# A three-stage attention and feed-forward kernel: one transpose for the leftover keys of two query parts, quarter tiles in the fifth value step, and another order of all operations

## The chip, the cores and the metric

The kernel runs on one core of a Trainium2 chip. TensorE (PE in the rows; its weight loads are PEld) multiplies matrices, VectorE (DVE), ScalarE (ACT) and GpSimd (POOL) work elementwise, and SyncE (SP) issues most transfers. The metric is the device time of one execution in microseconds (us), the median of several runs.

## The reference, cut to what matters

```python
scores = scale * np.matmul(q, k.transpose(0, 1, 3, 2))      # 4 batches, 8 heads, 576 queries and keys, head size 64
thresh = np.max(scores, axis=-1, keepdims=True) - tau
scores = np.where(scores >= thresh, scores, -1000000000.0)
attn = np.exp(scores - np.max(scores, axis=-1, keepdims=True))
attn = attn / (np.sum(attn, axis=-1, keepdims=True) + 1e-09)
x = np.matmul(attn, v)                    # laid out as 2304 tokens x 512
h = x @ moe_w_in;   x = (h * np.clip(h + 3, 0, 6) / 6) @ moe_w_out                 # 512 -> 2048 -> 512
h = x @ moe2_w_in;  out = (h * (1 / (1 + np.exp(-1.702 * h)))) @ moe2_w_out        # 512 -> 2048 -> 512
```

## The kernel before

The kernel writes its work down as some five thousand operations, each with an engine, a planned cost, its buffers and a function that issues its instructions (`add`, `move`, class `Plan`). Many operations have an alternative engine (`alt`). `Plan.settle` runs a list scheduler over them: `order` keeps, for each engine, a heap sorted by a key, and starts whatever comes first and is ready by the planned costs and the latencies `LAT`. The emitted program is the operations in the order of their planned starts. Each engine then executes its own list strictly in that order, and semaphores keep the dependencies. The costs are the writer's formulas: a one-input GpSimd operation on n columns is put at `pool1(n)`, 124 + 1.042 n nanoseconds. In the kernel before, two long lists of seeds (`KICKS`, `SHAKES`) disturb the key and swap engines until the final order comes out.

Attention works in units of two heads, four units to a batch. Batch 0 (`half`) is worked differently from batches 1 to 3 (`full`), which the change touches: 12 units in all. The 576 queries of a head are two parts, p = 0 with 256 queries and p = 1 with 320 (`CH`). One tile of scores is 128 queries by 576 keys. A unit has nine: two tiles for each head in each part, and a ninth (number 4, `tiles[4]` is None) with the last 64 queries of both heads. `score2` multiplies a tile on TensorE (L685); `soft` finds its maximum (DVE L733), the threshold (L734 or ACT L735), the exponentials (ACT L736), and masks and sums (DVE L737). `norm` multiplies the whole 576-column tile by the reciprocal sum (L750 on GpSimd, L753 on VectorE).

The weighted sum over values needs the keys on the partitions, so that the tiles have to be turned. 576 keys are four blocks of 128 and a leftover of 64. In part 0 (`blocks`) VectorE turns 32 by 32 blocks of the first 512 keys (L802) and two rounds of transfers finish the turn; in part 1 (`turn`) TensorE transposes them, 128 by 128 at a time (L791). The leftover 64 keys of the four tiles of each part go through TensorE in both parts: four transposes with 64 output rows, and one copy out of PSUM (L794 on ScalarE, L795 on VectorE). The upper 64 rows of the target are zeroed once for all units (L1246, L1247). Then `av_` multiplies (L850): for each part five steps of 128 keys (the fifth half zeros), and in each step one multiplication for each of the two heads. A head has 64 value columns, so the two heads lie side by side in the array. The names: `e` and `er` are tiles of attention weights (er the ninth), `et` the turned weights, `kqv` a buffer of keys, queries or values, `pm` a PSUM bank, `xr` the result.

Between and after these units run the two feed-forward layers in split form (a high and a low part of each operand, three multiplications a product): L910, L935, L1025 and L1136. Their weights arrive as 64-bit numbers and are decoded by `decode`: ScalarE takes the magnitude (L528), then a maximum and a minimum are applied (L529 on VectorE, or its alternative L530 on GpSimd), VectorE shifts (L531) and adds the sign (L532), GpSimd adds the low word, and `split` makes the high and low parts (`inhring`, `inlring`, `outhring`, `outlring`). The staging tile is `wmstg`. L478 and L475 are helper lines that many elementwise operations share. Where the planner leaves TensorE idle, `fill` puts in dummy multiplications (L1303).

```python
        def pool1(n):
            return 124 + 1.042 * n
...
        add(DVE, 335, time, "W", lambda: nc.vector.tensor_scalar(out=t.t, in0=t.t, scalar1=2.0 ** -15, scalar2=MOST, op0=ALU.max, op1=ALU.min), [], [t], (),
            (POOL, pool1(DM), lambda: nc.gpsimd.tensor_scalar(out=t.t, in0=t.t, scalar1=2.0 ** -15, scalar2=MOST, op0=ALU.max, op1=ALU.min)))
```

Of the kernel before, what the change touches and what calls it, by code (L numbers as in the profile page):

```python
# [9 lines left out]
F32 = mybir.dt.float32  # L10
# [8 lines left out]
P = 128  # L19
# [12 lines left out]
PORT = {DVE: {"W", "XHB", "XLB", "XD", "XLC", "GT2", "GL", "qs", "N", "kl", "XL", "XH", "GH", "kh", "qh", "ql"}, POOL: {"kl", "qs", "ql", "vl", "W", "GD", "N", "RM", "EL", "XL", "XLC", "GL"}}  # L32

KICKS = (
    1066518432, 520434182, 607402147, 51636981, 155525685, 845670547, 33034277, 701254722, 228382444, 659205109,
)

SHAKES = (
# [67 lines left out]
class Plan:  # L106
# [145 lines left out]
    def latest(self):  # L252
# [27 lines left out]
        return out  # L280

    def settle(self):

        self.link()
        self.order([float(o.time) for o in self.ops])
        for _ in range(3):
            key = self.latest()
            length = self.order(key)
# [43 lines left out]
def kicked(key, length, seed, kinds, count, ref=None):  # L332
# [6 lines left out]
    for _ in range(4):  # L339
        draw()  # L340
# [1021 lines left out]
```

## Time and profile before

| | |
|---|---|
| median of 3 runs | 1057.41 us (1056.98 to 1058.03) |
| span of the profiled execution, first to last instruction | 1054.9 us |
| TensorE busy | 1040.5 us (99%) |
| VectorE, ScalarE, GpSimd busy | 754.5, 618.5, 493.0 us |

The profiled execution has no time of its own beside its span; the three runs lie 2.1 to 3.1 us above that span, which is what starting and ending an execution adds outside the first and the last instruction. An engine's busy time is the union of its instructions. A matmul of full 32-bit numbers shows as two instructions of TensorE, a transpose as one. An instruction's duration contains its pipeline, so that neighbours overlap: what one costs on the path is the distance from its start to that of the next.

### The profile page before, as it was taken

The numbers are of one execution on the slowest core, as the hardware profiler recorded it, in microseconds if no ns is written. First come the engines' busy times: TensorE is split into PE (matmuls) and PEld (weight loads), VectorE is DVE, ScalarE is ACT, GpSimd is POOL, SyncE is SP. The second block draws the span as 40 slices with busy tenths as digits, with TensorE's granted clock in tenths as the row PEclk, the third lists the DMA queues.
The fourth block names the chain that finished last, engine by engine and source line by source line (L and its number), as shares of the span: only waits on it lengthen the run. The fifth ranks groups of instructions, "written<-read, shape, count | busy, mean of one in ns | idle before, by whom it ended". The sixth has DMA issues, their size and how long they took to land.

```text
span 1054.9 us, 19387 instructions
## 1 busy us (share of the span) xinstructions
PE 1040.5 (99%) x7066; PEld 948.2 (90%) x7066; DVE 754.5 (72%) x1539; ACT 618.5 (59%) x1228; POOL 493.0 (47%) x556
## 2 busy tenths in 40 slices
PE   8999999999999999999999999999999999999998
PEld 6686888899889998999999999989988998989988
DVE  7999889867888883677786426997687587464544
ACT  5989676566656664666454215655765566345433
POOL 5687877666757662755564226432331232001000
PEclk9999999999999999999999999999999999999999
DMA  7334465645564535445644213446553342321302
GB/s 231 121 113 137 147 181 162 183 137 160 161 184 132 148 115 162 137 144 167 203 145 145 84 43 111 135 139 200 165 191 120 125 159 78 115 88 33 96 2 74
DMA packets 83647, 141.71 MB, mean 134 GB/s; under 512 B 8160, under 2 KB 47712, under 8 KB 82016
## 3 DMA queue, kind: packets, MB, share of 16 engines
q1 hardware_dynamic: 83408, 140.18, 44.1%
q8 instruction: 56, 0.92, 0.4%
q14 instruction: 39, 0.32, 0.1%
q10 hardware_dynamic: 144, 0.29, 0.1%
HBM read 97.32 MB, written 43.12 MB: 133 GB/s over the span
## 4 chain that ended last, share of the span: by engine, by line
PE 88%; DVE 4%; ACT 2%; DMA 2%; SPq 1%; POOL 1%; issue 1%; DVEq 0%; ACTq 0%; POOLq 0%
PE py L935 26%; PE pm L1136 17%; PE pm L910 10%; PE pm L935 9%; PE pm L1025 7%; PE ps L685 6%; PE pm L850 6%; PE pm L791 4%; PE ps L717 1%; PE pm L833 1%; DMA kqv<-in_vp_dram 1%; DVE wmstg L532 1%; ACT et L794 1%; SPq L644 0%; DVE nm L733 0%
## 5 line engine op out<-in xcount | busy, mean ns | idle before, releaser
L935 PE MATMUL py<-g,outhring 128*128 128x512 f32 (+3 forms) x1024 | 279.1, 357 | 1.7 <-DVE yc L478 1.6
L935 PEld LDWEIGHTS py<-g,outhring 128*128 128x128 f32 x1024 | 178.0, 188 | 17.9 <-DVE yc L478 2.1
L935 PE MATMUL py<-g,outlring 128*128 128x512 f32 (+3 forms) x512 | 182.5, 356 | 0.0
L1136 PE MATMUL pm<-outhring,inhring 128*128 128x256 f32 x512 | 144.4, 282 | 0.0
L1136 PE MATMUL pm<-outlring,inhring 128*128 128x256 f32 x512 | 144.1, 282 | 0.2 <-DVE outlring L478 0.2
L1136 PE MATMUL pm<-outhring,inlring 128*128 128x256 f32 x512 | 143.9, 281 | 0.0
L733 DVE TENSOR_REDUCE nm<-ps 128x1 f32<-128x576 f32 x144 | 106.9, 752 | 31.1 <-PE ps L685 27.2
L478 POOL TENSOR_TENSOR wmstg<-wmstg,wrstg 128x512 uint32<-128x512 uint32 x48 | 68.0, 1417 | 93.3 <-DVE wmstg L532 59.5
L736 ACT ACTIVATE e<-ps,nm 128x576 f32<-128x576 f32 x128 | 93.0, 739 | 31.4 <-DVE nm L733 27.4
L737 DVE SCALAR_TENSOR_TENSOR e<-ps,th,e 128x576 f32<-128x576 f32 x128 | 102.3, 811 | 12.4 <-ACT e L736 9.9
L478 POOL TENSOR_TENSOR g<-t,g 128x256 fp32r<-128x256 f32 (+2 forms) x83 | 78.5, 952 | 65.3 <-ACT g L475 49.9
L478 POOL TENSOR_TENSOR g<-tc,g 128x512 fp32r<-128x512 f32 x24 | 32.0, 1334 | 164.2 <-ACT g L475 139.4
L935 PE MATMUL pm<-g,outhring 128*128 128x256 f32 (+1 forms) x512 | 106.9, 300 | 0.1
L935 PEld LDWEIGHTS py<-g,outlring 128*128 128x128 f32 x512 | 96.2, 188 | 11.0
L1136 PEld LDWEIGHTS pm<-outlring,inhring 128*128 128x128 f32 x512 | 96.8, 189 | 4.3 <-DVE outlring L478 0.5
L1136 PEld LDWEIGHTS pm<-outhring,inhring 128*128 128x128 f32 x512 | 96.7, 189 | 4.0
L910 PE MATMUL pm<-xh,inhring 128*128 128x256 f32 (+1 forms) x320 | 97.5, 305 | 0.2
L1136 PEld LDWEIGHTS pm<-outhring,inlring 128*128 128x128 f32 x512 | 97.5, 190 | 0.0
L910 PE MATMUL pm<-xh,inlring 128*128 128x256 f32 (+1 forms) x320 | 94.4, 295 | 0.0
L910 PE MATMUL pm<-xl,inhring 128*128 128x256 f32 (+1 forms) x320 | 94.4, 295 | 0.0
L935 PEld LDWEIGHTS pm<-g,outhring 128*128 128x128 f32 x512 | 82.0, 189 | 1.4 <-issue 0.9
L685 PE MATMUL ps<-kqv 128*128 128x288 f32 x480 | 81.2, 300 | 0.0
(139 smaller groups left out, 2453.9 us busy)
## 6 DMA issues: line engine op xcount, KB each, us to landing
turned<-tr SPq DMA_DIRECT2D x12, 1024.0 KB, 4.2
et<-turned SPq DMA_DIRECT2D x48, 256.0 KB, 6.3
wrawstg<-in_w1i_dram SPq DMA_DIRECT2D x16, 512.0 KB, 3.9
wrawstg<-in_w1o_dram SPq DMA_DIRECT2D x16, 512.0 KB, 3.6
wrawstg<-in_w2i_dram SPq DMA_DIRECT2D x16, 512.0 KB, 4.0
wrawstg<-in_w2o_dram SPq DMA_DIRECT2D x16, 512.0 KB, 3.7
qk<-in_k_dram SPq DMA_DIRECT2D x24, 288.0 KB, 4.1
qk<-in_q_dram SPq DMA_DIRECT2D x24, 288.0 KB, 3.6
```

The lines of the kernel that those rows point to most:

```text
L478: return lambda: (nc.vector if eng == DVE else nc.gpsimd).tensor_tensor(out=o(), in0=a(), in1=b(), op=op)
L532: add(DVE, 602, time, "W", lambda: nc.vector.scalar_tensor_tensor(out=tu(), in0=high(), scalar=0xC0000000, in1=tu(), op0=ALU.bitwise_and, ...
L685: nc.tensor.matmul(ps.t[:, i, :SH], qss[hd].t[:, q0:q0 + P], w[hd].t[:, i * SH:(i + 1) * SH], start=a, stop=z)
L733: add(DVE, 672, K("R", s), "R", lambda: nc.vector.tensor_reduce(out=nm.t[:, c], in_=ps.t[:, :, :SH], op=ALU.max, axis=AX.XY, negate=True), ...
L736: add(ACT, 624, K("X", s), "X", lambda: nc.scalar.activation(out=ev(), in_=ps.t[:, :, :SH], func=ACTF.Exp, bias=nm.t[:, c]), [ps, (nm, s)] ...
L737: add(DVE, 736, K("M", s), "M", lambda: nc.vector.scalar_tensor_tensor(out=ev(), in0=ps.t[:, :, :SH], scalar=th.t[:, c], in1=ev(), op0=ALU ...
L791: nc.tensor.transpose(pt.t[:kn, o:o + P], e_of[s].t[:, keys(k)], id_b.t)
L850: nc.tensor.matmul(pv[p].t[64 * hd:64 * hd + 64, :CH[p][1]], v_(k, hd), x, start=k == 0, stop=k == 4)
L910: nc.tensor.matmul(ph.t[:, :n], a, v, start=(cc == 0 and i == 0), stop=(cc == KC - 1 and i == 2))
L935: nc.tensor.matmul(py.t[:, :n], a, v, start=(st and i == 0), stop=(sp and i == 2))
L1025: nc.tensor.matmul(ph.t[:, :n], a, v, start=(cc == 0 and q == 0), stop=(cc == KC - 1 and q == 2))
L1136: nc.tensor.matmul(o.t[:, :n], u.t[:, ws], v.t[:, xv], start=(st and kk == 0 and i == 0), stop=(sp and kk == 1 and i == 2), skip_group_che ...
```

## The change

It has three parts. The line numbers behind an arrow are those of the changed kernel.

First, the leftover keys. In the 12 units of batches 1 to 3, `norm` no longer multiplies the whole tile at once: it does the first 512 columns in place and writes the last 64 columns into a packed buffer `pk` (L750 -> L784), in which the leftovers of a tile of part 0 and of the corresponding tile of part 1 lie side by side as 128 columns. `packed` transposes `pk` with four full transposes, so that part 0's leftover keys come out on partitions 0 to 63 and part 1's on 64 to 127. The two groups of four 64-row transposes, one for each part, become one group of four, and two copies out of PSUM become one. The ninth tile's leftover is transposed with the 64 keys before it, so that it lands on partitions 64 to 127. The two memsets of zeros go.

Second, the fifth value step. `av_` does four steps for each part as before (L850 -> L927), then four multiplications at the end (L931), each with 64 keys and 64 value columns, that is a quarter of the array: part 0 on partitions 0 to 63, part 1 on 64 to 127, the two heads on the two halves of the columns. Each of the two parts still has its own PSUM bank.

Third, the order. The seeds are replaced by a list of operations whose engine is swapped (`SWAPS`) and a table of ranks (`RANKS`), by which the same list scheduler sorts. Every engine's whole list changes. The program has 48 matmuls less (6,631 before, 6,583 now). Among the swaps: the maximum and minimum of the decoded weights stands on GpSimd 22 times (3 before) and on VectorE 42 times (61 before), the multiplication of the first 512 columns on ScalarE for 38 of 96 tiles, the thresholds on ScalarE 56 times (26 before), and the low parts of g on GpSimd 60 times (83 before). The counts of transfers are the same. `TURNED` is empty, so that `both` is False and part 1 is turned by TensorE (`turned_by_pe`) in every unit, as before.

```diff
...
+RANKS = """
...
+SWAPS = (
+    18, 22, 28, 33, 58, 68, 108, 128, 148, 168, 192, 197, 254, 259, 269, 274, 316, 326, 331, 360, 371, 393, 410, 430, 453, 517, 528, 542, 615, 619, 629, 633, 659, 667, 669, 683, 692,
...
     def settle(self):
...
+        for n in SWAPS:
+            op = self.ops[n]
+            (op.eng, op.cost, op.fn), op.alt = op.alt, (op.eng, op.cost, op.fn)
...
-        self.link()
+        key = [float(o.time) for o in self.ops]
+        ranks = b85decode("".join(RANKS.split()))
+        if ranks:
+            key = [float(ranks[i] + 256 * ranks[i + 1]) for i in range(0, len(ranks), 2)]
         self.order(key)
+        for _ in range(0 if ranks else 3):
+            self.order(self.latest())
         return sorted(self.ops, key=lambda o: (self.start[o.n], o.n))
...
     def et_4():
-        return ets[1].t[:, 2048:2560].rearrange("p (h n) -> p h n", h=2)
+        return ets[1].t[:, 2048:2688].rearrange("p (h n) -> p h n", h=2)
...
+        pk = None if early else buf("pk", 2, "tr", [P, 4, 2, 64])
...
             recip(ss, ss[-1])
             for s in ss:
-                def mul(s=s, e=e_of[s]):
-                    nc.gpsimd.tensor_scalar(out=e.t, in0=e.t, scalar1=rc.t[:, s:s + 1], scalar2=1.0, op0=ALU.mult, op1=ALU.mult)
-
-                def alone(s=s, e=e_of[s]):
-                    nc.vector.tensor_scalar(out=e.t, in0=e.t, scalar1=rc.t[:, s:s + 1], scalar2=1.0, op0=ALU.mult, op1=ALU.mult)
-
-                add(POOL, 724, K("N", ss[-1]), "N", mul, [(rc, s)], [e_of[s]], (), (DVE, 69 + 0.521 * S, alone))
+                t, e = tiles[s], e_of[s]
+
+                def mul(eng, o, i, s=s):
+                    return lambda: (nc.vector if eng == DVE else nc.gpsimd).tensor_scalar(out=o(), in0=i(), scalar1=rc.t[:, s:s + 1], scalar2=1.0, op0=ALU.mult, op1=ALU.mult)
+
+                n = 512 if t else S
+
+                def main(e=e, n=n):
+                    return e.t[:, :n]
+
+                add(POOL, pool1(n), K("N", ss[-1]), "N", mul(POOL, main, main), [(rc, s)], [(e, 0)] if t else [e], (),
+                    (ACT, act(n), lambda main=main, s=s: nc.scalar.activation(out=main(), in_=main(), func=ACTF.Copy, scale=rc.t[:, s:s + 1])))
+                if t:
+                    def to(t=t):
+                        return pk.t[:, 2 * t[0] + t[1] % 2, t[1] // 2]
+
+                    def of(e=e):
+                        return e.t[:, 512:]
+
+                    add(POOL, pool1(64), K("N", ss[-1]), "NR", mul(POOL, to, of), [(rc, s), (e, 1)], [(pk, t)], (), (DVE, 69 + 0.521 * 64, mul(DVE, to, of)))
...
-        def trans(parts, size, dst, et, tag, at):
-
-            pt = bank(0)
-            kn = {keys(k).stop - keys(k).start for _, k, _ in parts}.pop()
+        def trans(parts, size, dst, et, tag, at, kn=P, row=0):
+
+            pt, rd = bank(0), [x for _, b, _ in parts for x in b]
 
             def tr():
-                for s, k, o in parts:
-                    nc.tensor.transpose(pt.t[:kn, o:o + P], e_of[s].t[:, keys(k)], id_b.t)
-
-            add(PE, len(parts) * 110, K("T", at), "T", tr, [id_b] + [e_of[s] for s in sorted({x[0] for x in parts})], [pt], [et])
-            add(ACT, act(size), K("EH", at), "EH", lambda: nc.scalar.activation(out=dst(kn)[0], in_=dst(kn)[1](pt.t[:kn, :size]), func=ACTF.Copy), [pt], [(et, tag)], (),
-                (DVE, dve(size), lambda: nc.vector.tensor_copy(out=dst(kn)[0], in_=dst(kn)[1](pt.t[:kn, :size]))))
-
-        def blocks(ss):
-
-            et, at, src = ets[1], ss[-1], buf("tr", 1, "tr", [P, 4, 2, 4, 2, 32])
+                for src, _, o in parts:
+                    nc.tensor.transpose(pt.t[:kn, o:o + P], src(), id_b.t)
+
+            add(PE, len(parts) * 110, K("T", at), "T", tr, [id_b] + rd, [pt], [et])
+            add(ACT, act(size), K("EH", at), "EH", lambda: nc.scalar.activation(out=dst()[0], in_=dst()[1](pt.t[row:kn, :size]), func=ACTF.Copy), [pt], [(et, tag)], (),
+                (DVE, dve(size), lambda: nc.vector.tensor_copy(out=dst()[0], in_=dst()[1](pt.t[row:kn, :size]))))
...
+        def cols(s, lo, n=P):
+            return (lambda: e_of[s].t[:, lo:lo + n]), [(e_of[s], int(lo >= 512))] if tiles[s] else [e_of[s]]
...
             for s in ss:
-                hd, t = tiles[s]
-                add(DVE, 626, K("DT", s), "DT", lambda hd=hd, t=t, e=e_of[s]: nc.vector.transpose(out=src.t[:, :, hd, :, t, :].rearrange("p g k j -> p k g j"), in_=e.t[:, :512].rearrange("p (k g j) -> p k g j", k=4, g=4)),
-                    [e_of[s]], [(src, s)])
-            turned, there = turns[u % 2]
-            move(K("DM", at), "DM", 16 * P * 512, lambda: nc.sync.dma_start(out=turned, in_=src.t.rearrange("p g h k t j -> p (g h k t j)")), [src], [there])
+                hd, t = tiles[s][0], tiles[s][1] % 2
+                add(DVE, 626, K("DT", s), "DT", lambda hd=hd, t=t, e=e_of[s]: nc.vector.transpose(out=at_(hd, t), in_=e.t[:, :512].rearrange("p (k g j) -> p k g j", k=4, g=4)),
+                    [(e_of[s], 0)], [(src, s)])
+            there, mk = turns[u % 2 * 2 + p]
+            move(K("DM", at), "DM", 16 * P * 512, lambda: nc.sync.dma_start(out=there, in_=src.t), [src], [mk])
...
+        def packed(at):
+
+            et = ets[1]
+            parts = [(lambda i=i: pk.t[:, i].rearrange("p a n -> p (a n)"), [pk], i * P) for i in range(4)]
...
+                trans(parts, 512, lambda: (et_4()[:, :, :256], lambda x: x.rearrange("p (h n) -> p h n", h=2)), et, (0, 4), at)
+            trans([(*cols(4, S - P), 0)], P, lambda: (et_4()[64:, :, 256:], lambda x: x.rearrange("p (h n) -> p h n", h=2)), et, "r4", at, row=64)
...
+                trans([(*cols(4, k * P), k * P) for k in range(4)], 512, lambda: (et_m(1, turned)[:, :, :, 256:].rearrange("p h k n -> p k h n"), lambda x: x.rearrange("p (k h n) -> p k h n", k=4, h=2)), et, "r", at)
...
             def mm():
                 for p in range(2):
-                    for k in range(5):
+                    for k in range(4):
                         for hd in range(2):
-                            x = et_a(et, 1, hd, k) if p else et_4()[:, hd] if k == 4 else et_0()[:, :, hd, k].rearrange("p a t j -> p t a j")
-                            nc.tensor.matmul(pv[p].t[64 * hd:64 * hd + 64, :CH[p][1]], v_(k, hd), x, start=k == 0, stop=k == 4)
-
-            add(PE, 200 + 10 * (2 + 0.84 * S), K("AV", at), "AV", mm, [vs, et], pv, xrs.values())
+                            nc.tensor.matmul(pv[p].t[64 * hd:64 * hd + 64, :CH[p][1]], v_(k, hd), et_m(p, turned)[:, hd, k], start=k == 0, stop=False)
+                for p in range(2):
+                    for hd in range(2):
+                        r = slice(64 * p, 64 * p + 64)
+                        nc.tensor.matmul(pv[p].t[64 * hd:64 * hd + 64, :CH[p][1]], v_(4, hd)[r], et_4()[r, hd, :CH[p][1]], start=False, stop=True)
+
+            add(PE, 200 + 8 * (2 + 0.84 * S) + 733, K("AV", at), "AV", mm, [vs, et], pv, xrs.values())
...
-                if p:
-                    turn(p, ss, 4)
-                else:
-                    blocks(ss)
+                (blocks if p in turned else turned_by_pe)(p, ss)
+            packed(ss[-1])
...
-            add(POOL, 124 + 1.04 * 512, t, "ez", lambda: nc.gpsimd.memset(et_4()[64:], 0.0), [], [(ets[1], (0, 4))])
-            add(POOL, 124 + 2.08 * 320, t, "ez", lambda: nc.gpsimd.memset(et_all(ets[1], 1)[64:, :, 4, :], 0.0), [], [(ets[1], x) for x in ((1, 4), "r4")])
```

On TensorE, in the first unit of batch 1, the transposes of part 0's leftover keys and those of part 1's are these in the kernel before (the row with 64x128 and x4 is a leftover group; e is a tile of weights, and xh, xl and the ring tiles are the operands of the feed-forward layer between them):

```order
L791 MATMUL pm<-id,e 128x128 x8
L791 MATMUL pm<-id,e 64x128 x4
L791 MATMUL pm<-id,e 128x128 x4
L910 MATMUL pm<-xh_743,inhring_389 128x320
L910 MATMUL pm<-xl_749,inhring_389 128x320
L910 MATMUL pm<-xh_743,inlring_402 128x320
L791 MATMUL pm<-id,e 128x128 x4
```

In the changed kernel the same stretch has this, where pk is the packed buffer of both parts:

```order
L835 MATMUL pm<-id,e 128x128 x4
L1014 MATMUL pm<-g,outhring_1393 128x256 x2
L1014 MATMUL pm<-g,outlring_1422 128x256
L835 MATMUL pm<-id,pk 128x128 x4
L1014 MATMUL pm<-g,outhring_1519 128x256 x2
L1014 MATMUL pm<-g,outlring_1557 128x256
```

The 64-row groups are gone, and one group of four full transposes of pk has come.

The value product of that unit stands on TensorE before the change as follows, between score products of the next unit (L685) and the feed-forward layer:

```order
L910 MATMUL pm<-xh_743,inhring_468 128x320
L910 MATMUL pm<-xl_749,inhring_468 128x320
L910 MATMUL pm<-xh_743,inlring_487 128x320
L850 MATMUL pm<-et,kqv 64x256 x10
L850 MATMUL pm<-et,kqv 64x320 x10
L685 MATMUL ps<-kqv 128x288 x4
```

And after it:

```order
L709 MATMUL ps<-kqv 128x288 x8
L927 MATMUL pm<-et,kqv 64x256 x8
L927 MATMUL pm<-et,kqv 64x320 x8
L931 MATMUL pm<-et,kqv 64x256 x2
L931 MATMUL pm<-et,kqv 64x320 x2
L709 MATMUL ps<-kqv 128x288 x8
```

Two of the ten multiplications of each part have moved to the end as quarter tiles, behind both parts' full steps.

On GpSimd, among the weights of the first layer (in batch 0, while the second to fourth tiles of weights are decoded), the list before is:

```order
L478 TENSOR_TENSOR wmstg<-wmstg,wrawstg 128x512
L478 TENSOR_TENSOR inlring_487<-wmstg,inhring_468 128x512
L771 TENSOR_SCALAR bt<-rc 128x128 x2
L478 TENSOR_TENSOR xl_507<-xr_411,xh_489 128x256
L478 TENSOR_TENSOR wmstg<-wmstg,wrawstg 128x512
L743 TENSOR_SCALAR sm<-sm 128x4
L478 TENSOR_TENSOR inlring_559<-wmstg,inhring_548 128x512
L478 TENSOR_TENSOR xl_584<-xr_509,xh_577 128x256
```

and after it (L547 is the line of the maximum and minimum on GpSimd, L530 before):

```order
L495 TENSOR_TENSOR inlring_505<-wmstg,inhring_499 128x512
L775 TENSOR_SCALAR sm<-sm 128x4
L547 TENSOR_SCALAR wmstg<-wmstg 128x512
L495 TENSOR_TENSOR wmstg<-wmstg,wrawstg 128x512
L816 TENSOR_SCALAR bt<-rc 128x128 x2
L495 TENSOR_TENSOR xl_590<-xr_512,xh_582 128x256
L495 TENSOR_TENSOR inlring_607<-wmstg,inhring_584 128x512
L495 TENSOR_TENSOR wmstg<-wmstg,wrawstg 128x512
L547 TENSOR_SCALAR wmstg<-wmstg 128x512
```

Of the 22 such rows, 8 stand among the sixteen weight tiles of the first layer's first half, and 14 among the later weights. Before the change one of its 3 stood there.

## Rows read from the trace of the kernel before

**Rows 1.** The page: span, busy time of each engine, shares of the closing chain.

```profile
span 1054.9 us, 19387 instructions
...
PE 1040.5 (99%) x7066; PEld 948.2 (90%) x7066; DVE 754.5 (72%) x1539; ACT 618.5 (59%) x1228; POOL 493.0 (47%) x556
...
PE 88%; DVE 4%; ACT 2%; DMA 2%; SPq 1%; POOL 1%; issue 1%; DVEq 0%; ACTq 0%; POOLq 0%
```

**Rows 2.** Busy time by stretch: from:to in us, length, then each engine, clock, DMA.

```profile
0.00:25.00 25.00, 21.03 (x114) 16.55 (x115) 19.42 (x53) 13.86 (x23) 13.25 (x32) 1.00 0.80 232
25.00:130.00 105.00, 101.57 (x739) 81.07 (x738) 96.50 (x227) 88.84 (x178) 82.58 (x102) 1.00 0.43 129
130.00:410.00 280.00, 278.16 (x2138) 250.80 (x2138) 225.52 (x546) 182.26 (x362) 186.92 (x261) 1.00 0.56 159
410.00:530.00 120.00, 118.23 (x866) 114.98 (x862) 83.27 (x151) 70.64 (x143) 68.05 (x55) 1.00 0.53 162
530.00:1000.00 470.00, 469.79 (x2861) 436.55 (x2860) 308.37 (x519) 243.53 (x481) 140.87 (x108) 1.00 0.38 120
1000.00:1055.00 55.00, 51.77 (x361) 48.23 (x360) 21.39 (x44) 19.41 (x44) 1.29 (x1) 0.99 0.11 37
```

**Rows 3.** Waits: engine and line, whom for, us in total, times, longest.

```profile
PE py L935 <- DVE yc L478: 1.6, 1, 1.6
...
PE pm L935 <- POOL outlring L478: 1.0, 1, 1.0
...
ACT xr L475 <- PE pm L850: 33.5, 19, 2.9
```

**Rows 4.** The closing chain in order of time: start, length on the path, what.

```profile
40.53 2.31 PE pm L833 x20
...
61.57 1.17 PE ps L717 x8
...
68.53 2.84 PE pm L833 x20
...
71.92 0.97 PE ps L717 x4
...
181.43 5.00 PE pm L850 x40
...
405.94 2.18 PE pm L791 x20
```

**Rows 5.** Timeline of TensorE: start, length to the last end, line, shapes.

```profile
61.50 1.24 PE L717 MATMUL ps<-kqv 64*128 64x288 f32 x8
...
71.76 1.13 PE L717 MATMUL ps<-kqv 128*128 128x288 f32 x4
...
228.27 0.60 PE L791 MATMUL pm<-id,e 128*64 128x128 f32 x4
228.63 0.48 PE L935 MATMUL pm<-g,outhring 128*128 128x256 f32 x2
```

**Rows 6.** Groups by line and shape: count, busy us, mean ns, idle before.

```profile
L530 POOL TENSOR_SCALAR wmstg<-wmstg 128x512 f32<-128x512 f32 x3 | 6.0, 1987 | 5.8 <-ACT wmstg L528 3.1 <-DVE tc L478 2.7
...
L750 POOL TENSOR_SCALAR e<-e,rc 128x576 f32<-128x576 f32 x88 | 66.5, 766 | 12.0 <-DVE rc L744 10.3 <-PE pm L791 0.4
...
L529 DVE TENSOR_SCALAR wmstg<-wmstg 128x512 f32<-128x512 f32 x61 | 35.6, 585 | 20.3 <-ACT wmstg L528 20.3
...
L794 ACT ACTIVATE et<-pm 128x512 f32<-128x512 f32 x89 | 51.0, 597 | 12.6 <-PE pm L791 11.9
L794 ACT ACTIVATE et<-pm 64x512 f32<-64x512 f32 x28 | 16.4, 585 | 1.8 <-PE pm L791 1.7
```

**Rows 7.** VectorE around 503 us, then the chain from there to TensorE's wait.

```profile
503.58 1.51 DVE L531 TENSOR_SCALAR wmstg<-wmstg 128x512 uint32<-128x512 uint32 x1 [3.20 <-POOL wmstg L530]
...
502.79 0.77 POOL wmstg L530
...
513.84 0.41 DVE yc L478
...
514.29 1.83 PE py L935 x13
```

More of the change, by code (lines that the diff above doesn't have):

```diff
@@ L1 @@
-import random
+from base64 import b85decode
 from contextlib import ExitStack
@@ L329, in fill @@
         return out
-def kicked(key, length, seed, kinds, count, ref=None):
-    def draw():
-        nonlocal seed
-        seed = (seed * 6364136223846793005 + 1442695040888963407) & 0xFFFFFFFFFFFFFFFF
-        return (seed >> 33) / 2147483648.0
-    for _ in range(4):
-        draw()
-    widths, odds = ((2e4, 6e4, 2e5, 2e6), 3) if ref is None else ((1e3, 4e3, 1.2e4, 4e4), 2)
-    size, width = (100.0, 300.0, 1000.0, 3000.0)[int(draw() * 4)], widths[int(draw() * 4)]
-    lo = draw() * (length + width / 2) - length - width / 2
-    noise, kind = int(draw() * 4) < odds, int(draw() * count)
-    shift = (draw() * 2 - 1) * size * 3
-    out = list(key)
-    for o, r in enumerate(ref or key):
-        if lo <= r < lo + width:
-            if noise:
-                out[o] += (draw() + draw() - 1) * 2 * size
-            elif kinds[o] == kind:
-                out[o] += shift
-    return out
 @with_exitstack
@@ L380, in tile_top_attention_moe_moe2 @@
     FULL = 4
+    TURNED = {}
     scale = 0.125
@@ L596, in tile_top_attention_moe_moe2 @@
     QC = S + 64
-    turns = [(dram.tile([P, 2048], F32, name="turned"), mark()) for _ in range(2)]
+    turns = [(dram.tile([P, 2048], F32, name="turned"), mark()) for _ in range(4)]
     ets = [buf("et", 1, "et", [P, 10 * S]) for _ in range(2)]
@@ L616, in unit @@
     def unit(u, b, j, t0):
-        early = u < FULL
+        early, turned = u < FULL, TURNED.get(u, (0,))
+        both = len(turned) == 2
+        pk = None if early else buf("pk", 2, "tr", [P, 4, 2, 64])
         tiles = [(0, 0), (1, 0), (0, 1), (1, 1), None, (0, 2), (1, 2), (0, 3), (1, 3)]
@@ L680, in score2, with mm @@
             ps, t = buf("ps", 2, "ps", [P, 2, 512]), tiles[s]
-            def mm(hd, q0, st, sp):
+            def mm(hd, q, st, sp):
                 for w, a, z in ((khs, st, False), (kls, False, sp)):
                     for i in range(2):
-                        nc.tensor.matmul(ps.t[:, i, :SH], qss[hd].t[:, q0:q0 + P], w[hd].t[:, i * SH:(i + 1) * SH], start=a, stop=z)
+                        nc.tensor.matmul(ps.t[:, i, :SH], q, w[hd].t[:, i * SH:(i + 1) * SH], start=a, stop=z)
             def run():
                 for hd in range(2) if t is None else t[:1]:
-                    mm(hd, t[1] * P + 128 * hd if t else 0 if hd else 512, t is not None or hd == 0, t is not None or hd == 1)
+                    if t is None:
+                        q = slice(0, P) if hd else slice(512, 512 + P)
+                        mm(hd, qss[hd].t[:, q], hd == 0, hd == 1)
+                    else:
+                        q0 = t[1] // 2 * 256 + 128 * hd
+                        if both:
+                            mm(hd, qss[hd].t[:, q0 + t[1] % 2:q0 + 256:2], True, True)
+                        else:
+                            mm(hd, qss[hd].t[:, q0 + t[1] % 2 * P:q0 + t[1] % 2 * P + P], True, True)
             add(PE, (4 if t else 8) * pe(SH), K("S", s), "S", run, [x[hd] for hd in (range(2) if t is None else t[:1]) for x in (qss, khs, kls)], [ps])
@@ new lines, in cols, with blocks, at_ @@
+        def cols(s, lo, n=P):
+            return (lambda: e_of[s].t[:, lo:lo + n]), [(e_of[s], int(lo >= 512))] if tiles[s] else [e_of[s]]
+        def blocks(p, ss):
+            et, at, src = ets[1], ss[-1], buf("tr", 1, "tr", [P, 2048])
+            def at_(hd, t):
+                if both:
+                    return src.t.rearrange("p (g h k j t) -> p k g h j t", g=4, h=2, k=4, t=2)[:, :, :, hd, :, t]
+                return src.t.rearrange("p (g h k t j) -> p k g h t j", g=4, h=2, k=4, t=2)[:, :, :, hd, t, :]
+            for s in ss:
+                hd, t = tiles[s][0], tiles[s][1] % 2
[3 more added lines that the diff above has]
+            move(K("DM", at), "DM", 16 * P * 512, lambda: nc.sync.dma_start(out=there, in_=src.t), [src], [mk])
+            for g in range(4):
+                move(K("DM", at) + 3000, "DM", 7 * P * 512, lambda g=g: nc.sync.dma_start(out=ets[1].t[32 * g:32 * g + 32, 2688 * p:2688 * p + 2048].rearrange("p (a n) -> p a n", a=4),
+                     in_=there[:, 512 * g:512 * g + 512].rearrange("(a p) n -> p a n", a=4)), [mk], [(et, (p, ("m", g)))])
@@ L814, in turn, with turned_by_pe @@
+        def turned_by_pe(p, ss):
             for hd in range(2):
```

155 lines of the change are left out of this document (114 added, 41 removed), and 51 rows, old and new, of tables (SHAKES, SWAPS).

## The prediction, made before the changed kernel ran

> **What bounds the kernel now.** I read the page first. TensorE is busy for 1040.5 of 1054.9 us, and 88% of the chain that ended last is its work, while no other engine passes 72% [rows 1]. The table by stretch says where the other 14.4 us lie: 4.0 in the first 25 us, when the first tiles arrive, 3.4 from 25 to 130, 1.8 from 130 to 410 (the attention of batches 1 to 3), 1.8 from 410 to 530 and 3.2 at the end, when the last sums are stored [rows 2]. The clock stood at 1.00, the 2.4 GHz level, all the way (0.99 in the last stretch), so nothing below is clock [rows 2]. Hence an instruction taken off TensorE shortens the run by its step, as long as the operands of those behind it come earlier too; and a new order can take out no more than 7.2 us of waiting (3.4, 1.8, 1.8 and 0.2 between 530 and 1000), unless it shortens the start or the tail. The same table shows what is near its limit: VectorE is busy for 96.5 of the 105 us from 25 to 130, GpSimd for 82.6; from 130 to 410 it is 225.5 and 186.9 of 280.
>
> **What leaves TensorE: transposes.** Each of the 12 units loses one group of four. Twenty transposes take 2.18 us on the chain [rows 4], 0.109 each, and a group of four that stands between other matmuls moves the next one by 0.36 us, 228.27 to 228.63 [rows 5]. A transpose of 64 rows costs as much as one of 128, for the moving side has 128 columns either way. So 48 x 0.109 = 5.2 us, at least 12 x 0.36 = 4.3. I take 5.2, for most groups stand beside other transposes. The ninth tile's wider transpose costs the same as the old one.
>
> **What leaves TensorE: the fifth step.** A value product of 256 columns takes 2.31 us, one of 320 takes 2.84 (batch 0), and both together in a unit 5.00 [rows 4]. The difference, 2.31 + 2.84 - 5.00 = 0.15, is paid once for going into the two-column form. So a step of part 0 is (2.31 - 0.15)/5 = 0.43, one of part 1 (2.84 - 0.15)/5 = 0.54, and the fifth steps cost 0.97 together. Quarter tiles appear nowhere in this trace. If all four run side by side, the step lasts as long as its longer part, 0.54, and a change of form comes on top. For its price the nearest row is the score product of batch 0: eight instructions on 64 rows, which run in pairs, take 1.17 us, and four on all 128 rows with the same columns 0.97 [rows 4, 5]. Half the array beside the other half is thus free, but the form costs 0.20. I take 0.54 + 0.20 = 0.74 instead of 0.97: 0.23 a unit, 12 x 0.23 = 2.8 us. The bounds: no price for the change of form, 12 x 0.43 = 5.2 us saved; or only two quarters at a time, 0.97 + 0.20 = 1.17, which loses 12 x 0.20 = 2.4 us.
>
> Two rules of the Trainium skill bear on this step and disagree. "TensorEngine Tiling (Array Packing)", section Tiling Modes (Key Properties), says that a change of the tiling mode drains the engine. "TensorE: Matmul & The Clock Gate", part 3 (Measured speedup vs the span model), puts a pack of tiles at one matmul plus some 4 ns for each further tile; that would make the step 0.55 us and the saving about 5.0 us, an estimate by that page. The rows above side with the first: the form has a price.
>
> **What is added elsewhere.** The multiplication by the reciprocal sum was 88 GpSimd instructions of 0.77 us [rows 6] and is now 58 there of 512 columns, 38 on ScalarE (0.60 by the nearest 512-column row) and 96 small ones of 64 columns. Twelve copies out of PSUM of 0.59 go [rows 6]. In 130 to 410 us GpSimd has 93 us free and ScalarE 98 [rows 2], so I cost this at nothing; without that cover the 38 x 0.60 = 23 us of ScalarE would count. Part 0's result was finished half-way through the product and now ends with part 1's. The copy behind it (ScalarE waited for L850 33.5 us in 19 waits [rows 3]) starts up to 2.7 us later, but ScalarE stood and waited for part 1 there already. Cost nothing. Transfers are the same in number and size.
>
> **What the new order changes in the waits.** This is the part that no row prices directly. The new order may take out what TensorE waits for now, 7.2 us at most. It also puts 19 more maximum-and-minimum steps of the weights on GpSimd. There one takes 1.99 us, against 0.59 on VectorE [rows 6]; the planner's formula for it, 124 + 1.042 x 512, says 0.66. Each of them is some 1.3 us later than the plan believes, and the next step of the same weights stands on VectorE in a fixed place, with the softmax and the sums of the feed-forward layer queued behind it. The trace has one such case from end to end: GpSimd's L530 before 503.56 us, VectorE idle for 3.20 us until it was done, and at the end of that chain the sum yc at 513.84 and TensorE's wait before 514.29, 1.6 us, its longest [rows 3, 7]. Three uses, one of which cost 1.6: at that rate 19 more cost 10 us. The rate comes from a single case, and VectorE also gets 19 x 0.59 = 11 us less to do. Bounds for all waits together: 7.2 less, 10 more. I take 2.5 us more, a quarter of the upper end, because from 530 us on GpSimd and VectorE are far from full [rows 2].
>
> **The sum.** -5.2 - 2.8 + 2.5 = -5.5 us on the profiled span of 1054.9. The runs lie above that span by a constant part outside the program, so I take the same difference from the median: 1057.4 - 5.5 = 1051.9 us.
>
> **Rivals.**
> 1. GpSimd's slow step decides, the rival on the other side. Between 25 and 130 us seven more of them add 7 x 1.99 = 13.9 us to GpSimd, whose idle time there is 22.4 us, most of it inside the chains of the same weights, and TensorE already waits 1.0 us there for a low part that GpSimd makes (outlring) [rows 2, 3]. VectorE, 92% busy there, cannot make up for a late hand-over. If all of it reached TensorE, the time would be 1057.4 - 8.0 + 13.9 = 1063.3. It eats the gain to within 0.2% from 5.9 us on (8.0 - 2.1), and makes the kernel slower by more than that from 10.1 on. Against it: VectorE loses 4.1 us of the same work there, and the idle time is larger than the addition.
> 2. The quarters run two at a time: 5.2 saved, 2.4 lost, 2.5 of waits, 1057.1. For it: no row shows four. Against it: halves by rows and halves by columns both run side by side [rows 4, 5].
> 3. The new order also takes waits out: 8.0 and half of the 7.2, 1045.8. For it: most of these waits are single ones behind an engine that was a microsecond late [rows 3]. Against it: the old order had been fitted to the same formulas.
> 4. The work that leaves TensorE comes back as waiting, because from 25 to 410 us VectorE sets the pace: 1057.4. For it: 92% and 81% busy [rows 2]. Against it: TensorE was idle for 1.8 of 280 us from 130 to 410.
>
> **How the numbers follow.** A difference under 0.2% (2.1 us) is about what a measurement of this kernel can't tell from none. The forecast (waits between 0 and 5 us more, 1049.4 to 1054.4) gets 0.55; rival 1, from 5 us of waits on, 0.14 (0.03 of it still faster, 0.06 the same, 0.05 slower); rival 2 0.10 (0.05 faster, 0.04 the same, 0.01 slower); rival 3 0.17, all faster; rival 4 0.04, the same. Together faster 0.80, the same 0.14, slower 0.06. The range 1046.5 to 1057.2 leaves out the better part of the waits' lower bound below (0.07) and the worse half of rivals 1 and 2 above (0.11).
>
> **What would show it.** In the changed kernel's profile: 12 groups of four pk transposes and no 64-row group in batches 1 to 3; the eight instructions of L931 within 0.7 to 0.8 us of the last full step, four starts within some 20 ns of each other (rival 2: two and two, 1.2 us); L547 at 1.9 to 2.0 us on GpSimd, 22 times, with VectorE's waits for it longest between 25 and 130 us; TensorE's idle time from 25 to 530 us, 7.0 now, at 7 to 12 (rival 1: over 12, rival 3: under 5). The prediction is wrong if TensorE's own work falls by clearly less or more than 8 us, or if the order adds waits at a place that has no part in this, such as the start or the tail.

## Result, and the profile after

The changed kernel takes 1069.58 us (median of 4, 1067.23 to 1072.56) beside 1057.49: ratio 1.0118, 95% interval 1.0104 to 1.0132. It is slower by 12 us, where the forecast was 1051.9, faster, and the range ended at 1057.2. Rival 1 had the mechanism and the sign, but not the place nor the size.

The page of the changed kernel, span and busy time:

```profile
span 1068.5 us, 19325 instructions
...
PE 1043.2 (98%) x7018; PEld 941.7 (88%) x7018; DVE 783.8 (73%) x1619; ACT 620.7 (58%) x1233; POOL 486.2 (46%) x553
```

TensorE is idle for 1068.5 - 1043.2 = 25.3 us instead of 14.4 [rows 1], and it is busy for 2.7 us more although it has 48 instructions of transposes less to do. The same stretches as in [rows 2]:

```profile
0.00:25.00 25.00, 20.80 (x110) 15.96 (x111) 16.92 (x43) 12.65 (x23) 14.68 (x33) 1.00 0.77 226
25.00:130.00 105.00, 97.74 (x681) 75.52 (x680) 93.08 (x213) 84.70 (x168) 89.12 (x98) 0.97 0.36 107
130.00:410.00 280.00, 278.10 (x2146) 248.38 (x2144) 249.72 (x612) 202.52 (x404) 169.19 (x273) 1.00 0.59 167
410.00:530.00 120.00, 117.90 (x860) 113.86 (x860) 89.24 (x167) 61.57 (x121) 64.73 (x48) 1.00 0.51 153
530.00:1000.00 470.00, 463.35 (x2782) 427.40 (x2782) 306.79 (x533) 235.33 (x466) 144.58 (x100) 0.99 0.38 119
```

Two stretches changed: from 25 to 130 us TensorE is idle for 7.3 us (3.4 before), and from 530 to 1000, where it had waited for 0.2, for 6.6. Start and tail are as before. In the same two stretches the mean clock is below 1.00. A finer cut shows how (TensorE alone: busy time, clock, DMA):

```profile
50.50:54.00 3.50, 3.49 (x13) 0.52 0.60 183
...
118.90:122.30 3.40, 3.40 (x16) 0.50 0.00 0
675.40:678.70 3.30, 3.30 (x15) 0.50 0.15 30
695.60:698.90 3.30, 3.30 (x18) 0.52 0.60 187
...
90.90:96.90 6.00, 5.94 (x41) 1.00 0.20 40
```

Four times the clock stands at its 1.2 GHz level for 3.3 to 3.5 us, each time right behind a wait of TensorE of 1.6 to 1.9 us. The sum is 13.5 us at half speed; the same work takes half of that at 2.4 GHz, so about 6.7 us are lost. That is the rise in busy time, and more. Not every wait of this length is followed by it: in the same execution TensorE waited 1.80 us before 90.86 (last row) and 1.90 us before 764.54, and the clock stayed at 1.00.

What TensorE waits for (columns as in [rows 3]):

```profile
PE pm L1215 <- ACT p L492: 3.9, 3, 1.9
PE ps L709 <- DVE e L769: 2.7, 3, 1.9
PE py L1014 <- DVE g L495: 2.4, 6, 0.9
PE pm L911 <- DVE t L1001: 1.8, 1, 1.8
PE pm L1215 <- DVE outlring L495: 1.7, 1, 1.7
PE ps L749 <- DVE er L769: 1.6, 1, 1.6
```

Six different operands, none of them a weight's maximum-and-minimum step. But the step stands behind them. L547's row for GpSimd (minimum, median, maximum in ns), and the wait of VectorE that it makes:

```profile
L547 POOL TENSOR_SCALAR wmstg<-wmstg x22: 1914/1926/2304, 13.5 to 791.5; 128x512 f32<-128x512 f32 x22
...
DVE wmstg L548 <- POOL wmstg L547: 19.5, 17, 3.1
```

The chain of waits ahead of TensorE's wait at 118.32 us (start, length, what) has it in the open:

```profile
114.23 1.94 POOL wmstg L547
...
116.19 0.43 DVE wmstg L548
116.62 0.67 DVE nm L765
...
118.19 0.10 DVE e L769
...
118.32 0.40 PE ps L709
```

VectorE stands in a fixed order. L548 waits for GpSimd, and behind L548 stand the row maximum (L765) and the masking (L769) of a softmax that has nothing to do with those weights; the score product on TensorE needs the buffer that L769 frees.

At 674.63 us the step's part is less direct. The chain there goes back to a transfer, and from it to a product of TensorE:

```profile
660.89 2.91 PE pm L1104 x15
...
663.82 6.49 DMA xb<-x2d
...
673.97 0.61 DVE outlring L495
...
674.63 0.39 PE pm L1215
```

The timelines of VectorE, GpSimd and SyncE's queue before it, one under the other, then SyncE's wait, and the same two transfers in the run with the shortened step (below):

```profile
661.48 0.76 DVE L548 TENSOR_SCALAR wmstg<-wmstg 128x512 uint32<-128x512 uint32 x2 [1.06 <-POOL wmstg L547]
662.16 1.29 DVE L549 SCALAR_TENSOR_TENSOR wmstg<-wrawstg,wmstg 128x512 uint32<-128x512 uint32 x2
...
659.18 2.27 POOL L547 TENSOR_SCALAR wmstg<-wmstg 128x512 f32<-128x512 f32 x1
...
662.91 0.34 SPq L535 DMA_DIRECT2D wrawstg<-in_w2o_dram  x1
...
SPq L1151 <- PE pm L1104: 0.5, 1, 0.5
...
650.72 0.34 SPq L535 DMA_DIRECT2D wrawstg<-in_w2o_dram  x1
...
653.70 3.98 DMA xb<-x2d
```

GpSimd's step of 2.27 us holds up L548 for 1.06 us, then L549, which is the last reader of a raw weight buffer; SyncE waits for that buffer with the next weight load (L535). The load of xb (a tile of the first layer's result, read back from memory) stands behind it in the same queue, but it was not the queue that it waited for last: it went out when the product L1104 was done, as it did in the other run. What differs is its length, 6.49 us beside 3.98, and that is the whole delay: from its issue to L1215 it is 10.8 us here and 8.3 there. The weight load went out 0.9 us ahead of it here and 3.0 us there. That the two transfers were in each other's way, so that a late step on GpSimd became a longer transfer of something else, fits this; no run shows it alone.

### The profile page after: what moved, and what is told of

Read it like the earlier page. It is cut to its first block, busy times and chain, and to the rows that moved or that the text cites. A ratio compares the mean times of both kernels' runs of the same rounds, so it can differ in the third digit from the quotient of the medians.

```text
span 1068.5 us, 19325 instructions
## 1 busy us (share of the span) xinstructions
PE 1043.2 (98%) x7018; PEld 941.7 (88%) x7018; DVE 783.8 (73%) x1619; ACT 620.7 (58%) x1233; POOL 486.2 (46%) x553
## 4 chain that ended last, share of the span: by engine, by line
PE 77%; DVE 9%; POOL 5%; ACT 3%; issue 3%; DMA 2%; POOLq 0%; DVEq 0%; SPq 0%; ACTq 0%
PE py L1014 22%; PE pm L1215 16%; PE pm L989 8%; PE pm L1014 7%; PE ps L709 6%; PE pm L1104 6%; PE pm L927 5%; PE pm L835 4%; POOL wmstg L547 2%; PE pm L911 2%; PE ps L733 1%; PE ps L749 1%; DVE g L495 1%; DVE wmstg L549 1%; POOL wmstg L495 1%
## 5 line engine op out<-in xcount | busy, mean ns | idle before, releaser
L1215 PE MATMUL pm<-outhring,inhring 128*128 128x256 f32 x512 | 146.6, 286 | 4.2 <-ACT p L492 3.9
L1215 PE MATMUL pm<-outlring,inhring 128*128 128x256 f32 x512 | 145.0, 283 | 1.7 <-DVE outlring L495 1.7
L1215 PE MATMUL pm<-outhring,inlring 128*128 128x256 f32 x512 | 144.9, 283 | 0.0
L765 DVE TENSOR_REDUCE nm<-ps 128x1 f32<-128x576 f32 x144 | 106.5, 750 | 20.2 <-PE ps L709 16.0
L1215 PEld LDWEIGHTS pm<-outhring,inhring 128*128 128x128 f32 x512 | 97.9, 191 | 10.8 <-ACT p L492 5.8
L769 DVE SCALAR_TENSOR_TENSOR e<-ps,th,e 128x576 f32<-128x576 f32 x128 | 102.4, 810 | 4.5 <-ACT e L768 3.3
L1215 PEld LDWEIGHTS pm<-outlring,inhring 128*128 128x128 f32 x512 | 98.2, 192 | 5.3 <-DVE outlring L495 1.9
L495 POOL TENSOR_TENSOR g<-t,g 128x320 fp32r<-128x320 f32 (+2 forms) x60 | 57.8, 967 | 95.8 <-ACT g L492 85.3
L1215 PEld LDWEIGHTS pm<-outhring,inlring 128*128 128x128 f32 x512 | 98.6, 193 | 0.0
```

What stands on the lines that cost most here:

```text
L495: return lambda: (nc.vector if eng == DVE else nc.gpsimd).tensor_tensor(out=o(), in0=a(), in1=b(), op=op)
L765: add(DVE, 672, K("R", s), "R", lambda: nc.vector.tensor_reduce(out=nm.t[:, c], in_=ps.t[:, :, :SH], op=ALU.max, axis=AX.XY, negate=True), ...
L769: add(DVE, 736, K("M", s), "M", lambda: nc.vector.scalar_tensor_tensor(out=ev(), in0=ps.t[:, :, :SH], scalar=th.t[:, c], in1=ev(), op0=ALU ...
L1215: nc.tensor.matmul(o.t[:, :n], u.t[:, ws], v.t[:, xv], start=(st and kk == 0 and i == 0), stop=(sp and kk == 1 and i == 2), skip_group_che ...
```

## Experiments

All but the two new plans keep the order of the kernel that they start from; only the named instruction changes its engine, length or company. **Theory A**: GpSimd's L547, three times as long as the planner believes, makes the waits, and the waits bring the half-clock stretches. Its rivals are named with each run.

**All 22 steps on VectorE.** After the planner has fixed the order:

```
+        for op in self.ops:
+            if op.alt and op.alt[1] == 335 and op.eng == POOL:
+                op.fn = op.alt[2]
```

> The 22 maximum-and-minimum steps of the weights run on VectorE (about 0.43 us each, as L546 now) in the places of the same order that GpSimd's L547 (1.93 us) has now; nothing else moves. Theory A (GpSimd's slow step makes the waits, and the waits halve the clock): most of the 10.9 us of new waiting and of the 6.7 us that the four half-clock stretches cost go, 1069.6 - 9 - 6 = about 1054, clock 1.00. Rival B (the new order or the other swaps make the waits, the slow step only stands near them): 1066 or more, TensorE still idle for over 20 us.

Measured: 1055.10 us, ratio 0.9974 (0.9960 to 0.9989). Rival B falls: the order and the other swaps, with all that they moved, are still there, and the time is 14.5 us lower, which is more than the 12.1 us that the change had lost: the kernel is now 0.26% faster than the one before. The two stretches in its profile:

```profile
25.00:130.00 105.00, 99.77 (x721) 79.03 (x720) 98.37 (x231) 88.42 (x173) 81.79 (x100) 1.00 0.42 126
...
530.00:1000.00 470.00, 468.73 (x2860) 433.58 (x2859) 312.74 (x545) 238.32 (x475) 126.38 (x89) 1.00 0.37 118
```

TensorE's idle time is 5.2 and 1.3 us there. Of the ten executions the four at a mean clock of 1.00 took 1051.9 to 1053.5 us, the six at 0.995 to 0.998 took 1054.8 to 1057.5.

**The early steps or the late ones.** The same edit with `op.n < 1000`, or `op.n > 1000`, added to the condition.

> Only the 8 steps of the first layer's first weights (all before 130 us) go to VectorE; the 14 later ones stay on GpSimd. Theory A: the waits at 50.5, 90.9 and 118.3 us (1.6, 1.8 and 1.9) and the two half-clock stretches behind the first and the third (1.7 each) go: 1069.6 - 5.3 - 3.4 = about 1061. Rival B: no change, 1069.

> Only the 14 later steps (from 400 us on) go to VectorE; the 8 early ones stay on GpSimd. Theory A: the waits from 460 to 800 us (1.8 from 460 to 500, 0.8 from 500 to 560, 6.0 from 670 to 800) mostly go, and with them the two half-clock stretches at 675 and 696 (1.7 each): 1069.6 - 7 - 3.4 = about 1059. Rival B: no change, 1069.

Measured: 1063.49 us (1.0057, 1.0039 to 1.0074) and 1060.06 us (1.0013, 0.9998 to 1.0028). The eight early steps cost 6.1 us of the 1069.6, the fourteen later ones 9.5; together 15.6, close to the 14.5 of both at once. More than half of the loss comes from steps after 400 us. Nine of those fourteen run after 530 us, where the forecast had said that GpSimd and VectorE are far from full, and five before it; the two runs don't separate them. In the profiles TensorE's idle time from 530 to 1000 us is 6.6 us in the changed kernel and 1.7 with the later steps on VectorE.

**The kernel before with the steps.** The old order, the steps moved in place. The edit moves 20: the change had put 20 on GpSimd and taken one of the old three off, net 19, and that one stays here, so that 23 are on GpSimd:

```
+        steps = [o for o in self.ops if o.name == "W" and o.alt and 335 in (o.cost, o.alt[1])]
+        for k in (0, 1, 4, 5, 9, 11, 13, 15, 22, 24, 31, ...):
+            if steps[k].eng == DVE:
+                steps[k].fn = steps[k].alt[2]
```

> The kernel before, in its own order, with the 19 maximum-and-minimum steps that the change moved put on GpSimd in their places: one part of the change alone. Theory A: the waits come with them, by the rate of the changed kernel (about 9 us of waits and some half-clock stretches): 1064 to 1075. Rival B (the old order has room for them): 1057 to 1059.

Measured: 1074.63 us, 1.0163 (1.0148 to 1.0178), the upper end of what A expected: 17 us for these 20 steps alone. A plan that never heard of the steps suffers as much as the one that was searched with them at a wrong price.

**The steps shortened.** On GpSimd as in the changed kernel, but on 160 of the 512 columns (the others are not clamped):

```
-            (POOL, pool1(DM), lambda: nc.gpsimd.tensor_scalar(out=t.t, in0=t.t, ...
+            (POOL, pool1(DM), lambda: nc.gpsimd.tensor_scalar(out=t.t[:, :160], in0=t.t[:, :160], ...
```

> The changed kernel with its own order, and the 22 GpSimd steps shortened to 160 of their 512 columns (the other columns aren't clamped), about 1.93 x 160/512 = 0.6 us or a little more, which is near what the planner's formula says (0.66). Theory A (the price in the planner's formula is what is wrong, not the place of the steps): the waits go as with the steps on VectorE, 1052 to 1056. Rival D (any step of these on GpSimd costs a hand-over on a busy queue, however short): half of the loss stays, 1061 or more.

Measured: 1051.99 us, 0.9941 (0.9924 to 0.9958), all four executions at clock 1.00. GpSimd's row and VectorE's wait for it, then the two stretches:

```profile
L547 POOL TENSOR_SCALAR wmstg<-wmstg x22: 741/752/1369, 13.9 to 772.5; 128x160 f32<-128x160 f32 x22
...
DVE wmstg L548 <- POOL wmstg L547: 3.2, 6, 0.8
...
25.00:130.00 105.00, 99.85 (x724) 79.32 (x722) 98.05 (x228) 89.53 (x176) 87.58 (x107) 1.00 0.42 127
...
530.00:1000.00 470.00, 469.12 (x2865) 434.20 (x2864) 310.20 (x537) 239.04 (x475) 132.74 (x97) 1.00 0.37 118
```

Same engine, same places, same hand-overs, 0.75 us instead of 1.93: rival D falls. It is the length. That the time lands on the forecast's 1051.9 is luck: in this profile TensorE is busy for 6.6 us less than before, where the forecast had 8.0, and idle for 0.5 us more, where it had 2.5.

**TensorE kept busy in four of the waits.** In the function that puts in warm-up products, for the four instructions named by number:

```
+            if op.n in (536, 4452, 4510, 4776):
+                s = self.start[op.n]
+                spare = [i for i, u in enumerate(used) if not any(x < s and y > s - 600 for x, y in u)]
+                out += [make(i, 4) for i in spare[:1]]
```

> The changed kernel, with four of the kernel's own warm-up products (1.4 us of TensorE work on a free PSUM bank, results unused) put ahead of four of the instructions that wait longest: the score group at 50.5 us, the product at 674.6, those at 695.3 and 764.5. The late operands stay late. Theory A (the half-clock stretches are a second price of these waits: 3.3 to 3.5 us at half speed, 1.7 us lost each, and come only where TensorE stood still before): the stretches at 50, 675 and 696 us go, the clock at 118 may stay, 1069.6 - 2 to 5 = 1065 to 1067.5. Rival C (the clock falls for another reason, or the products push the queue back by what they take): 1069 or more.

Measured: 1067.19 us, 1.0087 (1.0058 to 1.0115). Its four executions: 1065.07 and 1065.23 at clock 1.00, 1069.16 and 1070.56 at 0.998 and 0.995. The profiled one is at 1.00 throughout, with late operands as before. No products stood ahead of the waits at 89 and 117 us, and the longer of them is still there:

```profile
116.84 1.85 PE L713 MATMUL ps<-kqv 128*128 128x288 f32 x12 [1.86 <-DVE e L773]
```

The clock stayed at 1.00 behind that one too, though nothing had been done about it. The median moved as A said, but its interval is wide. Here, as with all steps on VectorE, the executions at 1.00 are some 4 us faster than those below it, which is more than one fall costs. That idle time brings the half clock fits all the profiles, in which each fall inside the kernel stands right behind a wait of TensorE (1.53 to 2.55 us); this run doesn't settle it.

**The kernel before without its three.** The three steps that it had on GpSimd, on VectorE in their places.

> The kernel before, in its own order, with its three GpSimd steps on VectorE in their places. The prediction held the wait of 1.6 us at 514 us to be the price of one of them. Theory A: that wait goes, 1057.9 - 1.6 = 1056.3. Rival E (the reading of that one chain was wrong, another input would have been late anyway): 1057.9.

Measured: 1056.74 us, 0.9988 (0.9977 to 0.9999). The wait of 1.57 us at 514 us is 0.49 in its profile (at 512.35 us), so the reading of that chain was right for two thirds of it; the time moves by 0.6 us, at the edge of what can be told.

**Planned anew with the right price.** Swaps and ranks searched again, with this one number changed:

```
-            (POOL, pool1(DM), lambda: nc.gpsimd.tensor_scalar(...
+            (POOL, 1990, lambda: nc.gpsimd.tensor_scalar(...
```

> The changed kernel's computation, planned anew with one number of the planner changed: a maximum-and-minimum step on GpSimd costs 1.99 us instead of 0.66 (ranks and swaps searched again; the planner's own length becomes 1034.1 us, the changed kernel's was 1033.0 with the wrong price and is 1066.8 in the same rules with the right one). 15 of the steps stay on GpSimd, at other places. Theory A (a right price is enough; a slow step that the plan knows of costs nothing): about what the shortened step gave, 1049 to 1053, clock 1.00. Rival F (any long step on GpSimd between 25 and 800 us holds up VectorE, known or not): waits of 1 us and more behind L547 again, 1058 or more.

> A second plan, searched from another seed with the same price (planner's length 1034.6 us, 16 steps on GpSimd), to see whether the first stands for the rule or is one lucky order. Theory A: 1049 to 1053. Rival F: 1058 or more.

Measured: 1064.36 us (1.0055, 1.0035 to 1.0076) and 1064.39 us (1.0068, 1.0055 to 1.0081). The expectation was wrong. Rival F's time came out, its mechanism only in small part: VectorE's waits for the step (L536 there, first plan) are few, and no wait of TensorE is longer than 1.5 us, but there are many:

```profile
DVE wmstg L537 <- POOL wmstg L536: 4.2, 4, 1.5
...
PE ps L698 <- DVE e L758: 5.3, 11, 1.2
PE py L1003 <- DVE g L484: 3.7, 6, 1.2
...
25.00:130.00 105.00, 98.01 (x700) 75.92 (x699) 100.75 (x234) 82.65 (x162) 80.34 (x96) 1.00 0.39 119
130.00:410.00 280.00, 274.39 (x2095) 242.32 (x2095) 256.15 (x637) 198.72 (x392) 147.60 (x237) 1.00 0.58 161
```

In the first plan, above, VectorE is at 100.8 of 105 and 256.2 of 280 us (101.0 and 260.1 in the second), fuller than in the changed kernel's order, and TensorE waits 5.6 us from 130 to 410 where it waited 1.9. Two other seeds might do better. What the two show is that putting this one price right was not enough; that the new plans lean on other wrong prices is a guess, and why they are slower stays open.

**The step split.** 160 columns on GpSimd, 352 on VectorE at once, nothing left out:

```
+ lambda: [e.tensor_scalar(out=t.t[:, s], in0=t.t[:, s], ...)
+          for e, s in ((nc.gpsimd, slice(0, 160)), (nc.vector, slice(160, DM)))]
```

> The changed kernel in its own order, each of the 22 steps cut in two: 160 columns on GpSimd (0.75 us in the shortened run) and the other 352 on VectorE (about 0.3 us), the whole computation kept. Theory A: GpSimd's share ends about when the planner believes, VectorE gets 22 x 0.3 = 7 us over 800, so close to the shortened step and a little better than all on VectorE: 1052 to 1054, clock mostly 1.00. Rival G (VectorE between 25 and 130 us, 98 of 105 busy with all steps on it, has no room for a second instruction): as with all on VectorE, 1055 or more.

Measured: 1056.69 us, 0.9983 (0.9972 to 0.9994), not better than all on VectorE. GpSimd's share takes 0.80 us and VectorE's 0.39 (medians). Rival G's time came out, but not its reason: VectorE is busy for 97.9 of 105 us from 25 to 130, and it was for 98.05 with the shortened step, which is 4.7 us faster. Its later stretches:

```profile
130.00:410.00 280.00, 277.14 (x2139) 245.31 (x2141) 244.34 (x596) 197.55 (x396) 164.74 (x265) 1.00 0.57 160
...
530.00:1000.00 470.00, 466.89 (x2840) 432.08 (x2839) 312.30 (x545) 236.31 (x469) 131.57 (x97) 1.00 0.37 119
```

Of the 5.1 us that TensorE is idle more than with the shortened step, 0.4 lie between 25 and 130 us, 1.7 and 2.2 in these two. Why, stays open. Nor is the shortened step's lead over all steps on VectorE explained: the executions of both at a mean clock of 1.00 take the same (1051.0 to 1053.3 and 1051.9 to 1053.5 us); only the second has executions below it.

## Why the prediction was wrong

**What leaves TensorE** was right, term by term. A unit's product in the changed kernel, from the chain, and the timeline of the last step up to 275.83 us:

```profile
271.85 4.03 PE pm L927 x32
275.88 0.70 PE pm L931 x8
...
275.81 0.50 PE L931 MATMUL pm<-et,kqv 64*64 64x256 f32 x4
```

4.03 + 0.70 = 4.73 us instead of 5.00 [rows 4]: 0.27 saved a unit, 3.2 in all, where the forecast had 0.23 and 2.8. Four instructions start within 0.02 us, as the forecast had said of quarters that run side by side, and with 0.70 us instead of 1.17 rival 2 is out. "TensorE: Matmul & The Clock Gate", part 3 (Measured speedup vs the span model) of the Trainium skill would make the step 0.55 us, an estimate; it took 0.70, that is 0.16 more than the longer part's 0.54. "TensorEngine Tiling (Array Packing)" of the Trainium skill, section Tiling Modes, says that a change of mode drains the engine; the trace agrees in that the change has a price. Added up over the trace from each instruction's start to the next one's on TensorE, idle time taken off, the transposes take 55.0 us before (L791) and 50.0 in the shortened-step run (L835), at clock 1.00 all through: 5.0 saved, where the forecast had 5.2. So the two terms gave 8.2 of 8.0. TensorE's busy time fell by less, 6.6 us (1033.97), because the new order gave some back on other lines: by the same count the score products (L685, L701, L717) go from 99.3 to 100.8 us.

**What is added elsewhere** cost about nothing, as said: with the short step TensorE's idle time is 1048.9 - 1034.0 = 14.9 us, beside 14.4.

**The step that failed** is the one on the waits: "I take 2.5 us more, a quarter of the upper end, because from 530 us on GpSimd and VectorE are far from full". The working had the price from the row (1.99 us beside the formula's 0.66) and, from the one case in the trace, the rate: "at that rate 19 more cost 10 us". The idle time rose by 10.9. That the rate came so close is in part luck: it rests on one wait, and the kernel before without its three steps gained 0.6 us, not 1.6, while 20 more of them in its order cost 17. What was wrong was the discount. From 530 to 1000 us GpSimd was busy for 30% and VectorE for 66% [rows 2], and still 8 of the 17 waits of VectorE for L547, 9.8 of their 19.5 us, fell there, the longest among them. The sign that the forecast had set, TensorE's idle time from 25 to 530 us at 7 to 12, even came out, at 11.3; it left out the stretch where 6.6 us arose. A mean share of busy time says nothing of a fixed order: a hand-over that comes 1.3 us late holds up whatever stands behind it on the engine, as at 118 us, and idle time after that does not give it back to TensorE, which was 99% busy.

For the same reason rival 1, which had the mechanism, was drawn too small. It stopped at 130 us, where VectorE is full, and ended at 1063.3. The early steps cost 6.1 us and the later ones 9.5.

**The second thing left out** is the clock: "nothing below is clock". It was true of the trace before, where the longest wait is 1.6 us and no stretch falls. In the profiled execution of the changed kernel 1.7 us lost behind each of four waits make 6.7 us. That the waits bring the falls is likely, not shown. From the shortened step to the changed kernel the profiled spans differ by 19.6 us: 10.4 of idle time, 6.7 of half clock, and 2.5 of busy time that no row places.

The Trainium skill's "GPSIMD Engine Reference", section 4.1 (Engine selection), sends an elementwise maximum to VectorE but calls a one-input operation on GpSimd "roughly line-rate". The trace agrees with the first, and not with the second: 1.93 us against a median of 0.43 on VectorE for the same 128x512, which holds for this pair of operations (a multiplication is faster, see the last section).

Whether a correct version beats both: with all 22 steps on VectorE the kernel takes 1055.10 us, 0.9974 of before. The change was worth that, and 0.9941 with a step of 0.75 us, near what the planner believed, which however leaves out part of the computation.

## What to carry to other kernels

Before trusting a searched order, hold every price that it was searched with against the profile, and count how often the order uses the ones that are off: here one formula, 0.66 for 1.93 us, used 22 times instead of 3, turned a gain of 3 to 5 us into a loss of 12. Putting one price right in the plan is not the whole cure: two orders searched with 1.99 took 1064.4. An engine with idle time can still be late, and a late instruction costs what stands behind it in fixed queues; a mean share of busy time is no reason to discount such hand-overs. Where TensorE is nearly always busy, a wait may be paid a second time in clock.

## What the runs showed of the hardware that was not expected

The maximum-and-minimum step on GpSimd takes 1.926 us for 512 columns and 0.752 for 160, so 1.17 us for 352 columns or 3.3 ns each. The multiplication by the reciprocal sum takes 0.697 us for the same 512 columns:

```profile
L784 POOL TENSOR_SCALAR e<-e,rc x58: 685/697/1252, 118.2 to 406.5; 128x512 f32<-128x512 f32 x58
```

Both are one instruction of the same kind with one input and two operations (there times the reciprocal sum, then times 1.0), and the planner's formula, 0.66, is right for this one. Whether the maximum and minimum themselves make the difference no run shows alone.

The half clock came after waits of about 1.6 us, and not after each: behind the wait at 118 us it fell in the changed kernel (1.90 us) and stayed in the run with the late steps moved (1.87 us, same order up to there). Executions of one order differ in it: with all steps on VectorE 1051.9 to 1057.5 us, the faster ones at a mean clock of 1.00.

VectorE's operations with two inputs can be held up while GpSimd works on two inputs. Two timelines from the changed kernel:

```profile
687.89 0.68 DVE L495 TENSOR_TENSOR tc<-tc,c 128x512 f32<-128x512 f32 x1
...
690.81 1.79 DVE L495 TENSOR_TENSOR outlring<-xa,outhring 128x512 fp32r<-128x512 f32 x1
692.52 1.77 DVE L495 TENSOR_TENSOR tc<-tc,c 128x512 f32<-128x512 f32 x1
...
686.87 2.03 POOL L547 TENSOR_SCALAR wmstg<-wmstg 128x512 f32<-128x512 f32 x1 [0.64 <-ACT wmstg L545]
690.64 1.40 POOL L495 TENSOR_TENSOR wmstg<-wmstg,wrstg 128x512 uint32<-128x512 uint32 x1 [1.75 <-DVE wmstg L549]
692.01 1.74 POOL L495 TENSOR_TENSOR g<-tc,g 128x512 fp32r<-128x512 f32 x1
```

The two of 1.79 and 1.77 us take 0.68 to 0.69 us where GpSimd stands still. The first ends at 692.60, 0.56 us after GpSimd's operation ended at 692.04; the second at 694.29, 0.54 after 693.75. So they run one after the other, as "SBUF — State Buffer" of the Trainium skill, section Who interferes with whom, says of VectorE's operations with two inputs in SBUF beside a GpSimd operation that reads SBUF. By that rule the first row, beside L547, would have been held up as well; it took 0.68 us, so the trace agrees for GpSimd's operations with two inputs and not for L547. On the chain to the wait at 695 us these two take 3.5 us instead of 1.4, and VectorE had waited 0.36 us for L547 shortly before: that wait is made for the most part by the meeting of the two engines.
